# Attention, then two expert layers on one core: weight operands made on another engine, kept in DRAM for the second token sweep, and the gate rows and early routing re-spaced

## The chip, the cores and the metric

The kernel runs on one core of one Trainium2 chip. The metric is the device time of one execution in microseconds (us); a kernel's number is the median of its runs. One further execution was recorded by the hardware profiler; the rows below come from that one. Engines are named as the profile names them: PE (TensorE), PEld (its weight loads), DVE (VectorE), ACT (ScalarE), POOL (GpSimd), SP (SyncE, which here only issues DMAs).

## What is computed

Three layers in a row, cut here to what matters:

```python
x = linear_attention(q, k, v, lam)      # blocks with a decaying state; 1536 tokens of width 512
p = domain_probs / (domain_probs.sum(-1) + 1e-9)
out = 0
for e in range(4):                      # first expert layer: every token through every expert
    out += p[:, e:e+1] * (np.maximum(x @ w1[e], 0) @ w2[e])     # 512 -> 1024 -> 512
logits = out @ w_gate                   # second layer: 8 experts, one expert for each token
e_of = argmax(logits); gate = softmax(logits)[e_of]
y[mask] = gate[mask] * (np.maximum(out[mask] @ w1b[e], 0) @ w2b[e])
```

All of it in float32: each operand is split into a high and a low part in a shorter format, and a product is three matmuls (high by high, low by high, high by low).

## The kernel before

**Sweeps and units.** The first expert layer takes the tokens in two sweeps of 768 (`SW`, `TS`). In each sweep eight units run one after another, one for each half of the hidden width of each of the four experts: units k = 0 to 7 are the first sweep, 8 to 15 the second, and unit k + 8 needs the same weights as unit k. A unit has a first product (PE tiles `h` or `b`, then the hidden parts `ht`) and a second (`y`, added into `acc` token tile by token tile, six tiles a unit).

**Plain and fast units.** Units 0, 1, 8, 14 and 15 are plain: `moe1_group` takes 384 or 256 tokens at a time, four hidden chunks f (`h`), then token tiles (`y`); a callback `units(i)` places other work after each. Units 2 to 7 and 9 to 13 (`FAST`) form the first product from seven block products instead of eight; `fast_unit` runs 14 pieces (`line`), with `hook1(i)` after each, then six tiles `y`, with `hook2(j)` after each. The fast units need sums of blocks of tokens (`t1` to `t4`, made once a sweep in `tokens_steps` during units 1 and 8) and seven weight operands a unit: `a11`, `a12`, `a22` and the sums `s1` to `s4`.

**Making weight operands.** `load_piece` brings half a block (512 KB) into one of four `raw` buffers; `hi_lo` makes the parts: ACT copies the high one, DVE or POOL subtracts for the low one. For plain blocks and for all `w1` blocks (`split_plain`) the low part alternates between POOL and DVE. For the blocks of fast units (`fast_steps`) four sums `s` are made on POOL, and seven pairs of parts by ACT and DVE. `split_to(w, k, most)` takes the next `most` of these steps from one list; where the hooks call it sets the order on every engine, since the program is written out in the order in which each engine executes (`manual_schedule`). SP issues each DMA in program order and waits there for its buffer.

**Routing ahead of time.** For the first six token tiles `acc` is final after the first sweep. During the second, DVE computes their gate logits (`logit_v`, 48 products of 512 elements, eight gate rows fetched as two lots of four into `x2`). In units 14 and 15 each of these tiles then goes through `route_choose` (argmax) and, two steps later, `route_send` (softmax, rank and scatter): a pipeline that `route_step` moves on once a slot, a slot being a hidden chunk or a token tile. All six enter in the six slots of unit 14's first group.

After the two sweeps comes the second expert layer, which the change does not touch.

Of the kernel before, what the change touches and what calls it, by code (L numbers as in the profile page):

```python
# [8 lines left out]
F32 = mybir.dt.float32  # L9
# [9 lines left out]
P = 128  # L19
# [21 lines left out]
FAST = [k for k in range(2, K1 - 2) if k != KS]  # L41

# [20 lines left out]
def body(ctx: ExitStack, tc: tile.TileContext, lam, att, dp, w1a, w2a, wg, wgt, w1b, w2b, out):  # L63
# [61 lines left out]
    order = {b: i for i, b in enumerate(blocks)}  # L125
    wt = {}
# [6 lines left out]
    def load_piece():  # L133
        i = state["load"]
        if i >= 2 * len(blocks):
            return
        state["load"] += 1
        (w, k), j = blocks[i // 2], i % 2
# [32 lines left out]
    def split_plain(n, c):  # L171
        i, b = 4 * n + c, blocks[n]
        if c == 0:
# [10 lines left out]
        hi_lo(hi, lo, t, V if i in (0, 3) or n >= ROUTED else G if i < 3 else los[i % 2])  # L184
# [6 lines left out]

    def fast_steps(n):
        k = blocks[n][1]
        ops = wt[0, k] = {}
        got = {"n": 0}
        HH = HF // 2

        def raw(d, f):
            return raw_q[0 if d == 0 or got.get("dropped") else 1][:, :, f * HH:f * HH + HH]

        def part(name, src):
            i = got["n"]
            got["n"] += 1
            if i % 2 == 0:
                x = "hl"[i // 2 % 2]
                got["t"] = wp.tile([P, 4, HF], F32R, tag=f"w0{x}", name=f"w0{x}_{k}_{i}")
            ops[name] = tuple(
                got["t"][:, 2 * (i % 2) + x, :].rearrange("p (c f) -> p c f", c=2)
                for x in range(2)
            )  # L210
# [16 lines left out]
        return [
            lambda: part("a11", raw(0, 0)),
            lambda: part("a12", raw(1, 0)),
            lambda: add("s1", raw(0, 1), raw(1, 1), ALU.add),  # L230
            lambda: add("s2", got["s1"], raw(0, 0), ALU.subtract),
            lambda: part("s2", got["s2"]),
            lambda: part("s1", got["s1"]),
            lambda: add("s3", raw(0, 0), raw(0, 1), ALU.subtract),
            s3,
            lambda: part("a22", raw(1, 1)),
            s4,
            lambda: part("s4", got["s4"]),
        ]

# [7 lines left out]
    def split_to(w, k, most=1):  # L248

        for _ in range(most):  # L250
# [3 lines left out]
            if step is None:  # L254
                steps_q[:0] = [(n, x) for x in fast_steps(n)]
# [200 lines left out]
    def moe1_mm2(k, hs, t0, j, midway=None):  # L456
# [10 lines left out]
        mm3(ps, parts, not midway, True)  # L467
# [9 lines left out]
    def open_fast():  # L477
        fx = st["fx"] = st_ctx.enter_context(pool("fx", 1, side="right"))
        st["sf"] = st_ctx.enter_context(pool("sf", 2, side="right"))
# [12 lines left out]
    def tokens_steps(g):  # L492
        def sums(d):
# [19 lines left out]
            return ([] if g else [whole]) + [  # L513
# [14 lines left out]
    def fast_unit(k, hook1, hook2):  # L528
# [101 lines left out]
    def logit_load(h):  # L630
        w = x2.rearrange("p d t -> p (d t)")[:, :4 * DM].rearrange("p (e d) -> p e d", e=4)
        SP.dma_start(
            out=w, in_=wgt[4 * h:4 * h + 4, :].unsqueeze(0).to_broadcast([P, 4, DM])
        )

    def logit_v(t, e):
        flat = x2.rearrange("p d t -> p (d t)")
        V.tensor_tensor_reduce(  # L638
            out=flat[:, 4 * DM:5 * DM], in0=acc[:, t, 0:DM],
            in1=flat[:, e % 4 * DM:e % 4 * DM + DM], scale=1.0, scalar=0.0,  # L640
            op0=ALU.mult, op1=ALU.add, accum_out=lg_v[:, t, e:e + 1],
        )

# [197 lines left out]
    with tc.manual_schedule():  # L841
# [150 lines left out]
        def plain_unit(k):  # L992
            todo = tokens_steps(k // KS)
            base = k // KS * TS
            for g in range(2):
                def units(i):
                    if g == 0:
                        split_to(1, k)
                    if g == 1:
                        split_to(0, k + 1, 2 if i < FC or i == FC + 2 else 1)  # L1000
                    if todo and (g or i > 1):
                        todo.pop(0)()

                moe1_group(k, base + g * TH, TH, units)
            while todo:
                todo.pop(0)()
            split_to(0, k + 1, 11)

        logits = []
        for k in range(1, K1 - 2):  # L1010
            if k not in FAST:
                plain_unit(k)
                if k == KS:
                    logit_load(0)
# [467 lines left out]
```

## Time and profile before

| what | value |
|---|---|
| median of 3 runs (lowest to highest) | 778.96 us (777.73 to 779.73) |
| profiled execution: its own time | 777.45 us |
| its span, first to last instruction | 775.7 us |
| PE busy | 751.4 us (97%) |
| DVE, ACT, POOL busy | 497.3, 323.7, 200.7 us |
| mean granted clock of PE | 0.992 of full speed |

The profiled execution is 1.5 us under the median; 1.75 us of it lie outside the span. Busy time is an average over stages with different limits, so it says where the time is but not what a change of one stage is worth.

### The profile page before, as it was taken

How to read it: one execution, taken by the hardware profiler on the slowest of the kernel's cores; microseconds unless marked ns; L12 is line 12 of the kernel's file. 1: busy time of each engine (PE TensorE's matmuls, PEld its weight loads, DVE VectorE, ACT ScalarE, POOL GpSimd, SP SyncE). 2: the span in 40 equal slices, each digit the busy share in tenths (PEclk: the TensorE clock that was granted, in tenths of full speed). 3: DMA queues.
4: the chain of work that ended last, by engine and by line, in shares of the span. 5: the costliest groups of instructions: out<-in, count | busy, mean ns of one | idle time of the engine just before them, and what ended most of it. 6: DMA issues, size and time to landing. Idle time of an engine off the chain costs nothing.

```text
span 775.7 us, 12531 instructions
## 1 busy us (share of the span) xinstructions
PE 751.4 (97%) x4736; PEld 673.9 (87%) x4736; DVE 497.3 (64%) x1039; ACT 323.7 (42%) x692; POOL 200.7 (26%) x176
## 2 busy tenths in 40 slices
PE   8999989999999999989999899998999999999995
PEld 7888879898898998878889697986998999998994
DVE  6443285665655657556876878758446876765883
ACT  3222334252443434344343342522123656655673
POOL 4563251221321212312222231234110113211013
PEclk9999999999999999999999999999999999999998
DMA  9765101211122122122213122187004685855660
GB/s 298 254 213 164 55 13 70 75 62 57 53 81 82 55 81 82 55 65 76 78 55 128 35 82 72 64 302 242 28 15 142 223 296 202 300 170 201 233 236 29
DMA packets 29993, 97.43 MB, mean 126 GB/s; under 512 B 3633, under 2 KB 5681, under 8 KB 29675
## 3 DMA queue, kind: packets, MB, share of 16 engines
q1 hardware_dynamic: 27819, 90.30, 34.4%
q0 software_dynamic: 2112, 6.31, 2.1%
q8 instruction: 38, 0.62, 0.3%
q14 instruction: 24, 0.20, 0.1%
HBM read 85.55 MB, written 11.24 MB: 125 GB/s over the span
## 4 chain that ended last, share of the span: by engine, by line
PE 64%; issue 18%; DVE 9%; ACT 3%; POOL 2%; DMA 2%; SPq 1%; POOLq 0%; ACTq 0%; DVEq 0%
PE y L430 33%; PE b L554 16%; PE h L430 8%; POOL out L110 2%; PE qk L325 1%; DVE x L638 1%; PE xo L384 1%; PE xo L378 1%; DVE w1l L169 1%; DMA att<-in_att 1%; DVE u L568 1%; PE z L1139 1%; ACT w1h L168 1%; DMA x<-in_wgt 1%; DVE w0l L169 1%
## 5 line engine op out<-in xcount | busy, mean ns | idle before, releaser
L471 DVE SCALAR_TENSOR_TENSOR acc<-y,p_sb,acc 128x512 f32<-128x512 f32 x84 | 62.9, 749 | 47.6 <-PE y L430 47.2
L169 POOL TENSOR_TENSOR w1l<-raw,w1h 128x512 fp32r<-128x512 f32 x32 | 42.8, 1338 | 177.3 <-ACT w1h L168 177.3
L169 DVE TENSOR_TENSOR w1l<-raw,w1h 128x512 fp32r<-128x512 f32 x96 | 69.3, 750 | 14.2 <-ACT w1h L168 14.2
L168 ACT CAST w1h<-raw 128x512 fp32r<-128x512 f32 x128 | 75.4, 617 | 0.0
L168 ACT CAST w0h<-raw 128x512 fp32r<-128x512 f32 x117 | 66.8, 618 | 0.7 <-DMA raw<-in_w1b 0.6
L110 POOL DMA_INDIRECT out<-y,xb x16 | 29.3, 1833 | 135.8 <-DVE y L1255 84.9
L430 PE MATMUL h<-xh,w0h 128*128 128x256 f32 (+1 forms) x208 | 58.8, 312 | 1.2 <-ACT w0h L168 1.2
L430 PE MATMUL h<-xh,w0l 128*128 128x256 f32 (+1 forms) x208 | 56.9, 302 | 0.0
L561 ACT COPY u<-b 128x384 f32<-128x384 f32 x66 | 31.5, 478 | 53.9 <-PE b L554 53.9
L169 DVE TENSOR_TENSOR w0l<-raw,w0h 128x512 fp32r<-128x512 f32 x74 | 49.4, 707 | 7.0 <-ACT w0h L168 6.6
L554 PE MATMUL b<-xh,w0h 128*128 128x384 f32 x176 | 48.9, 339 | 0.0
L568 DVE TENSOR_TENSOR u<-b,u 128x384 f32<-128x384 f32 x66 | 36.5, 553 | 18.8 <-ACT w1h L168 11.7
L215 POOL TENSOR_TENSOR s<-raw 128x512 f32<-128x512 f32 x11 | 15.8, 1437 | 117.6 <-DVE w0l L169 117.6
L430 PEld LDWEIGHTS h<-xh,w0h 128*128 128x128 f32 x208 | 38.8, 191 | 2.8 <-ACT w0h L168 1.4
L638 DVE CUSTOM_DVE_ANT_0 x<-acc,x 128x512 f32<-128x512 f32 x48 | 37.3, 776 | 3.3 <-DMA x<-in_wgt 3.1
L430 PEld LDWEIGHTS h<-xh,w0l 128*128 128x128 f32 x208 | 39.0, 191 | 0.4
L430 PE MATMUL g<-xg,w0h 128*128 128x288 f32 (+1 forms) x192 | 38.1, 293 | 0.0
L430 PE MATMUL h<-xl,w0h 128*128 128x256 f32 (+1 forms) x208 | 37.4, 302 | 0.0
L554 PEld LDWEIGHTS b<-xh,w0h 128*128 128x128 f32 x176 | 32.3, 188 | 0.5
L430 PEld LDWEIGHTS h<-xl,w0h 128*128 128x128 f32 x208 | 31.6, 191 | 0.0
L430 PEld LDWEIGHTS g<-xg,w0h 128*128 128x128 f32 x192 | 30.8, 189 | 0.0
L110 POOL DMA_INDIRECT bins<-acc,pos x12 | 12.4, 1033 | 68.3 <-DVE acc L726 37.4
(303 smaller groups left out, 2146.5 us busy)
## 6 DMA issues: line engine op xcount, KB each, us to landing
raw<-in_w2a SPq DMA_DIRECT2D x32, 512.0 KB, 3.3
raw<-in_w1b SPq DMA_DIRECT2D x32, 512.0 KB, 5.6
raw<-in_w2b SPq DMA_DIRECT2D x32, 512.0 KB, 4.7
raw<-in_w1a SPq DMA_DIRECT2D x30, 512.0 KB, 3.5
att<-in_att SPq DMA_DIRECT2D x24, 512.0 KB, 5.6
bins<-fill SPq DMA_DIRECT2D x1, 4626.0 KB
x<-in_wgt SPq DMA_DIRECT2D x2, 1024.0 KB, 5.1
xb<-bins SPq DMA_DIRECT2D x2, 578.2 KB, 6.7
```

The source lines that it names most:

```text
L110: i = G.indirect_dma_start(out=dst, out_offset=bass.IndirectOffsetOnAxis(ap=idx, axis=0), in_=src, in_offset=None, bounds_check=rows - 1, ...
L168: A.copy(out=hi, in_=src)
L169: eng.tensor_tensor(out=lo, in0=src, in1=hi.bitcast(F32), op=ALU.subtract)
L215: G.tensor_tensor(out=t, in0=a, in1=b, op=op)
L325: T.matmul(qk[r][:, h, :], kT[64 * r:64 * r + 64, h, :], qT[64 * r:64 * r + 64, h, :], start=True, stop=True,)
L378: T.matmul(xo[q, h, :], st[q, h, :], qd[q, h, :], start=h == 0, stop=False, skip_group_check=True,)
L430: T.matmul(ps, l, r, start=first and i == 0, stop=last and i == len(ops) - 1)
L471: V.scalar_tensor_tensor(out=acc[:, t, 0:DM], in0=ps, scalar=p_sb[:, t, e:e + 1], in1=acc[:, t, 0:DM], op0=ALU.mult, op1=ALU.add,)
L554: T.matmul(ps, l[:, d, c], r[:, d, :], start=first and i == 0, stop=i == len(ops) - 1, skip_group_check=not first,)
L561: A.copy(out=t, in_=bank[2, s])
L568: V.tensor_tensor(out=t, in0=bank[b, s], in1=t, op=ALU.add)
L638: V.tensor_tensor_reduce(out=flat[:, 4 * DM:5 * DM], in0=acc[:, t, 0:DM], in1=flat[:, e % 4 * DM:e % 4 * DM + DM], scale=1.0, scalar=0.0, ...
```

## The change

Five edits. (1) The four sums of a fast block are made on DVE instead of POOL, first in the list, and the seven parts come in another order and pairing (`PAIRS`). (2) From unit 2 on, all low parts of plain blocks are made on DVE. (3) The finished operands of units 2 to 5 are also written to DRAM (`kept`, four DMAs a unit, 3.5 MB); units 10 to 13 (`KEPT`) fetch them back into the operand tiles instead of loading raw weights and making the parts again. (4) Gate rows come one at a time into a ring of five places, and logits are computed in units 10 to 13 alone, three among the pieces and two after each token tile. (5) The early tiles enter the routing pipeline every second slot. Besides: token steps of plain units start at slot 0, hooks take their steps at other slots, and the first `y` tile of a fast unit uses the low hidden parts last (`late="l"`).

```diff
+KEPT = [k for k in FAST if k >= KS and k - KS in FAST]
+PAIRS = (("a11", "a12"), ("a22", "s2"), ("s1", "s3"), ("s4",))
+    loads = [(w, k) for w, k in blocks if w or k not in KEPT]
...
-        hi_lo(hi, lo, t, V if i in (0, 3) or n >= ROUTED else G if i < 3 else los[i % 2])
+        hi_lo(hi, lo, t, V if i in (0, 3) or n >= ROUTED else G if i < 3 else los[i % 2] if k < 2 else V)
...
             hi_lo(*ops[name], src, V)
+            if j == len(PAIRS[i]) - 1 and k in kept:
+                m = 2 * len(PAIRS[i])
+                SP.dma_start(out=kept[k][i, :, :m], in_=t[:, :m].bitcast(F32))
...
-            G.tensor_tensor(out=t, in0=a, in1=b, op=op)
+            V.tensor_tensor(out=t, in0=a, in1=b, op=op)
...
         return [
+            sums,
             lambda: part("a11", raw(0, 0)),
             lambda: part("a12", raw(1, 0)),
+            third,
             lambda: part("s2", got["s2"]),
+            fourth,
+            lambda: part("s3", got["s3"]),
             lambda: part("s4", got["s4"]),
         ]
+    def kept_steps(n):
...
+            SP.dma_start(out=t[:, :m].bitcast(F32), in_=kept[k - KS][i, :, :m])
...
-                        split_to(0, k + 1, 2 if i < FC or i == FC + 2 else 1)
-                    if todo and (g or i > 1):
-                        todo.pop(0)()
+                        split_to(0, k + 1, 2 if i == FC - 1 else 1)
+                    step = todo.pop(0) if todo else None
+                    if step:
+                        step()
...
-                    logits = [(t, e) for h in range(2) for t in range(TT) for e in range(4 * h, 4 * h + 4)]
+                    logits = [(t, e) for e in range(E2) for t in range(TT)]
...
-                if i % 3 == 1:
+                if i % 2 == 0:
                     split_to(1, k)
-                elif i % 3 == 0:
+                elif i < 6 and k in KEPT:
                     logit(1)
...
-                logit(1)
+                if k in KEPT:
+                    logit(2)
...
+        early = [x for t in range(TT - 2) for x in (t, None)] + [TT - 2, TT - 1]
...
-                moe1_group(k, t0, n, units, range(TT) if t0 == TS and k == KL - 1 else ())
+                moe1_group(k, t0, n, units, early)
```

What stands where now, at three places. First DVE in the second group of plain unit 8, from the low part of its first hidden chunk to that of its last (`ht_1152_0l` to `3l`; `t` and `t3l`, `t2l`, `t4l` are a token step, `w0..` operands of unit 9, `s_9` its sums). Before:

```order
L438 SCALAR_TENSOR_TENSOR ht_1152_0l<-h_1152_0_3194,ht_1152_0h 128x384
L169 TENSOR_TENSOR w0h_0_3211<-raw_2968,w0h_0_3211 128x512
L169 TENSOR_TENSOR w0h_0_3211<-raw_2990,w0h_0_3211 128x512
L509 TENSOR_TENSOR t_1_1_3216<-x_96 128x384
L169 TENSOR_TENSOR t3l<-t_1_1_3216,t3h 128x384
L438 SCALAR_TENSOR_TENSOR ht_1152_1l<-h_1152_1_3220,ht_1152_1h 128x384
L509 TENSOR_TENSOR t_1_1_3241<-t_1_1_3216,x_96 128x384
L169 TENSOR_TENSOR t2l<-t_1_1_3241,t2h 128x384
L438 SCALAR_TENSOR_TENSOR ht_1152_2l<-h_1152_2_3245,ht_1152_2h 128x384
L169 TENSOR_TENSOR w0l_2_3262<-s_9_3239,w0l_2_3262 128x512
L169 TENSOR_TENSOR w0l_2_3262<-s_9_3237,w0l_2_3262 128x512
```

And now:

```order
L470 SCALAR_TENSOR_TENSOR ht_1152_0l<-h_1152_0_3222,ht_1152_0h 128x384
L229 TENSOR_TENSOR s_9_3239<-raw_2988,raw_3010 128x512
L229 TENSOR_TENSOR s_9_3241<-s_9_3239,raw_2988 128x512
L541 TENSOR_TENSOR t_1_1_3243<-x_100,t_1_1_3218 128x384
L172 TENSOR_TENSOR t4l<-t_1_1_3243,t4h 128x384
L470 SCALAR_TENSOR_TENSOR ht_1152_1l<-h_1152_1_3247,ht_1152_1h 128x384
L172 TENSOR_TENSOR w0h_0_3264<-raw_2988,w0h_0_3264 128x512
L470 SCALAR_TENSOR_TENSOR ht_1152_2l<-h_1152_2_3267,ht_1152_2h 128x384
L172 TENSOR_TENSOR w0h_0_3264<-raw_3010,w0h_0_3264 128x512
L470 SCALAR_TENSOR_TENSOR ht_1152_3l<-h_1152_3_3286,ht_1152_3h 128x384
```

Three token steps between the chunks became one; the other steps moved to the group before, where each of the four chunks now carries one. Second, DVE in unit 10 from the hidden part of piece (5, 1) to the start of the last sums (`x_96,lg_v` is a logit). Before:

```order
L438 SCALAR_TENSOR_TENSOR ht_111l<-u_10_3721,ht_111h 128x384
L638 ISA x_96,lg_v<-acc,x_96 128x512
L638 ISA lg_v 128x1
L438 SCALAR_TENSOR_TENSOR ht_100l<-b_10_3624,ht_100h 128x384
L169 TENSOR_TENSOR w1l_3644<-raw_3470,w1h_3643 128x512
L438 SCALAR_TENSOR_TENSOR ht_101l<-b_10_3634,ht_101h 128x384
L568 TENSOR_TENSOR u_10_3665<-b_10_3692,u_10_3665 128x384
```

And now:

```order
L470 SCALAR_TENSOR_TENSOR ht_111l<-u_10_3717,ht_111h 128x384
L470 SCALAR_TENSOR_TENSOR ht_100l<-b_10_3616,ht_100h 128x384
L470 SCALAR_TENSOR_TENSOR ht_101l<-b_10_3629,ht_101h 128x384
L600 TENSOR_TENSOR u_10_3661<-b_10_3687,u_10_3661 128x384
```

The logit and the low part of `w1` went to earlier pieces. Third, SP from the last loads ahead of unit 10 to the fetch for unit 11, now (before, each pair `raw<-in_w1a` stood where a lot of `kept` stands, and one `x<-in_wgt` of 2048 behind the second pair):

```order
L266 DMA w0h_0_3538<-kept_88 128x2048
L266 DMA w0l_1_3540<-kept_88 128x2048
L266 DMA w0h_2_3556<-kept_88 128x2048
L266 DMA w0l_3_3558<-kept_88 128x1024
L156 DMA raw_3653<-in_w2a 128x1024
L156 DMA raw_3696<-in_w2a 128x1024
L266 DMA w0h_0_3787<-kept_89 128x2048
L266 DMA w0l_1_3789<-kept_89 128x2048
L266 DMA w0h_2_3807<-kept_89 128x2048
L266 DMA w0l_3_3809<-kept_89 128x1024
L672 DMA x_100<-in_wgt 128x512 x2
```

Behind every fetch of four stand only loads for units further ahead and gate rows that are used more than a unit later.

## Rows read from the trace of the kernel before

**Rows 1.** Chain that ended last, in order of time: start, us, what.

```profile
122.59 14.69 PE b L554 x84
137.28 16.85 PE y L430 x72
...
366.34 0.60 DVE w1l L169
...
564.06 5.61 PE y L430 x24
...
583.93 5.75 PE h L430 x48
```

**Rows 2.** Busy time by stretch: start:end, length, PE, PEld, DVE, ACT, POOL; clock, DMA.

```profile
85.81:102.72 16.91, 16.91 (x85) 15.26 (x84) 7.97 (x13) 5.21 (x10) 6.87 (x7) 1.00 0.09 31
102.72:122.42 19.70, 17.43 (x85) 15.19 (x84) 16.07 (x24) 8.05 (x16) 9.98 (x7) 1.00 0.16 54
122.42:153.97 31.55, 31.55 (x158) 28.25 (x157) 19.24 (x29) 12.48 (x25) 7.86 (x6) 1.00 0.15 52
311.67:350.11 38.44, 36.36 (x169) 31.42 (x168) 21.22 (x33) 16.08 (x31) 9.07 (x6) 0.96 0.21 71
382.80:415.50 32.70, 32.12 (x157) 28.09 (x156) 26.23 (x52) 12.52 (x25) 8.20 (x6) 1.00 0.18 65
415.50:450.30 34.80, 32.34 (x158) 28.07 (x156) 26.25 (x52) 12.50 (x25) 8.18 (x6) 1.00 0.26 91
482.96:514.53 31.57, 31.57 (x157) 28.23 (x156) 20.34 (x39) 12.82 (x26) 9.74 (x18) 1.00 0.38 127
514.53:543.90 29.37, 25.92 (x156) 22.02 (x155) 22.16 (x100) 8.68 (x28) 11.51 (x10) 0.94 0.82 277
```

**Rows 3.** Timeline of unit 9, DVE, POOL and one weight load of PE.

```profile
362.47 1.28 POOL L215 TENSOR_TENSOR s<-raw,raw 128x512 f32<-128x512 f32 x1
362.69 1.48 DVE L438 SCALAR_TENSOR_TENSOR ht_111l<-u,ht_111h 128x384 fp32r<-128x384 f32 x1 [0.59 <-ACT ht_111h L437]
363.83 1.49 POOL L215 TENSOR_TENSOR s<-s,raw 128x512 f32<-128x512 f32 x1
364.09 1.77 DVE L638 CUSTOM_DVE_ANT_0 x<-acc,x 128x512 f32<-128x512 f32 x1
366.40 0.19 PEld L430 LDWEIGHTS y<-w1h,ht_100l 128*128 128x128 f32 x1 [0.68 <-DVE ht_100l L438]
```

**Rows 4.** Timeline of unit 13, DVE: the same two operations without POOL beside them.

```profile
495.53 0.56 DVE L438 SCALAR_TENSOR_TENSOR ht_111l<-u,ht_111h 128x384 fp32r<-128x384 f32 x1 [0.59 <-ACT ht_111h L437]
496.00 0.68 DVE L638 CUSTOM_DVE_ANT_0 x<-acc,x 128x512 f32<-128x512 f32 x1
```

**Rows 5.** Chain of waits within unit 8, second group.

```profile
335.89 0.48 DVE t L509
...
336.39 0.52 ACT t2h L168
...
336.94 0.56 DVE t2l L169
337.50 0.47 DVE ht_2l L438
```

**Rows 6.** Busy time by stretch, of two us each.

```profile
344.00:346.00 2.00, 2.00 (x6) 1.57 (x5) 0.69 (x1) 0.49 (x1) 0.00 (x0) 0.50 0.00 0
522.36:524.37 2.01, 1.88 (x9) 1.39 (x10) 1.77 (x15) 0.53 (x2) 0.00 (x0) 1.00 1.15 345
```

**Rows 7.** Timeline of unit 11: DVE at the second lot of gate rows.

```profile
426.42 0.69 DVE L638 CUSTOM_DVE_ANT_0 x<-acc,x 128x512 f32<-128x512 f32 x1 [2.06 <-DMA x<-in_wgt]
```

**Rows 8.** Timeline of units 14 and 15, first groups.

```profile
534.39 0.17 PE L701 MATMUL rank<-oh,upper 128*128 128x8 bf16 x1 [2.46 <-DVE oh L673]
535.86 2.29 DVE L169 TENSOR_TENSOR w1l<-raw,w1h 128x512 fp32r<-128x512 f32 x1
```

**Rows 9.** Page, part 6: DMA issues, KB each, median us from issue to landing.

```profile
x<-in_wgt SPq DMA_DIRECT2D x2, 1024.0 KB, 5.1
```

More of the change, by code (lines that the diff above doesn't have):

```diff
@@ L134, in load_piece @@
         i = state["load"]
[L135 removed]
+        if i >= 2 * len(loads):
             return
         state["load"] += 1
[L138 removed]
+        (w, k), j = loads[i // 2], i % 2
         if k < K1:
@@ L183, in split_plain, with pair_of @@
             hi, lo = hi[:, c, :], lo[:, c, :]
-        hi_lo(hi, lo, t, V if i in (0, 3) or n >= ROUTED else G if i < 3 else los[i % 2])
+        hi_lo(hi, lo, t, V if i in (0, 3) or n >= ROUTED else G if i < 3 else los[i % 2] if k < 2 else V)
         if c % 2 == 1:
             drop_raw()
+    kept = {
+        k: dram.tile([len(PAIRS), P, 4, HF], F32, name=f"kept{k}") for k in FAST if k + KS in KEPT
+    }
+    def pair_of(t, j):
+        return tuple(
+            t[:, 2 * j + x, :].rearrange("p (c f) -> p c f", c=2) for x in range(2)
+        )
     def fast_steps(n):
@@ L194, in fast_steps @@
         ops = wt[0, k] = {}
-        got = {"n": 0}
+        got = {}
         HH = HF // 2
+        d0, d1 = raw_q[:2]
         def raw(d, f):
-            return raw_q[0 if d == 0 or got.get("dropped") else 1][:, :, f * HH:f * HH + HH]
+            return (d0, d1)[d][:, :, f * HH:f * HH + HH]
         def part(name, src):
[L202 to L205, printed above, removed]
+            i, j = next((i, p.index(name)) for i, p in enumerate(PAIRS) if name in p)
+            if j == 0:
+                x = "hl"[i % 2]
@@ L232, in fast_steps, with fetch @@
             lambda: part("s2", got["s2"]),
[L233 to L237, printed above, removed]
+            fourth,
+            lambda: part("s3", got["s3"]),
             lambda: part("s4", got["s4"]),
         ]
+    def kept_steps(n):
+        k = blocks[n][1]
+        ops = wt[0, k] = {}
+        def fetch(i):
+            x = "hl"[i % 2]
+            t = wp.tile([P, 4, HF], F32R, tag=f"w0{x}", name=f"w0{x}_{k}_{i}")
+            names = PAIRS[i]
+            m = 2 * len(names)
+            SP.dma_start(out=t[:, :m].bitcast(F32), in_=kept[k - KS][i, :, :m])
+            for j, name in enumerate(names):
+                ops[name] = pair_of(t, j)
+        return [lambda i=i: fetch(i) for i in range(len(PAIRS))]
@@ L466, in moe1_mm2 @@
             parts = parts[FC // 2:]
-        mm3(ps, parts, not midway, True)
+        mm3(ps, parts, not midway, True, late)
         if k % KS == 0:
@@ L588, in fast_unit @@
             q, o = divmod(j * P, TH)
-            moe1_mm2(k, [hs[q, f] for f in range(FC)], t0 + q * TH, o // P)
+            moe1_mm2(
+                k, [hs[q, f] for f in range(FC)], t0 + q * TH, o // P, late="r" if j else "l"
+            )
             hook2(j)
```

69 lines of the change are left out of this document (36 added, 33 removed).

## The prediction

> **What bounds the kernel now.** I read the stretches between the starts of units first. PE is the bound wherever nothing holds it: a plain group of 384 tokens takes 16.91 us with PE busy throughout, a fast unit of the first sweep 31.55 us, the same; so does unit 13 with 31.57 [rows 2]. The chain of waits gives the two halves of a fast unit, 14.69 and 16.85 us [rows 1]. Against these lengths the other stretches show what PE lost:
>
> - unit 1, second group: 19.70, lost 2.8 [rows 2];
> - unit 8, both groups: 38.44 instead of 33.82, lost 4.6 [rows 2];
> - units 9, 10 and 12: 32.7 each (unit 10 is shown, the others are within 0.04), lost 1.15 each, and unit 11 34.80, lost 3.25: together 6.7 [rows 2];
> - the first groups of units 14 and 15: 29.37. Undisturbed groups further on have 5.75 + 5.61 = 11.36 [rows 1], two of them 22.7, and some 0.3 of rank matmuls stays: lost 6.35 [rows 2].
>
> Together 20.5 us, all in stretches that the change edits. In each, timelines and chain name DVE as what PE waits for: a hidden low part in unit 9 [rows 3], the chain through token steps in unit 8 [rows 5], the choice `oh` in unit 15 [rows 8]. The first sweep's six fast units lose nothing, so edits there can only cost.
>
> **Why DVE is late.** In unit 9 two sums `s` run on POOL from 362.47 on; the low part beside them takes 1.48 us and the logit behind it 1.77, and PE's load waits for the next low part [rows 3]. In unit 13, whose successor needs no sums, the same two operations take 0.56 and 0.68 [rows 4], and the unit loses nothing, though it has logits too. So 2.0 us of DVE's time are waits for POOL, and they cost 1.15 of PE's. Which instructions suffer is told by the rows as well: those with both inputs in SBUF. The Trainium skill, page "SBUF — State Buffer", section "Who interferes with whom", says that the second read port is shared, held for a whole instruction, and that a DVE instruction with two SBUF inputs blocks against a POOL instruction that reads SBUF. By that rule a sum moved to DVE cannot meet anything, since no POOL arithmetic is left after unit 1; the rows agree (1.77 beside 0.68), and the 2.0 would vanish whole. Were the port merely shared in proportion, part of it would stay with the added DVE work; that belongs to the second rival.
>
> **The change part by part.**
>
> *Sums and low parts to DVE (edits 1, 2).* Per fast unit four sums and two low parts more, about 0.6 us each by the low part in the chain [rows 1]: 3.6 us. A first-sweep unit has DVE busy for 19.24 of 31.55 [rows 2], some 2 of it waits of the above kind; afterwards about 21. PE hides it. Were that cover gone, it would cost at most 3.6 in each of six units.
>
> *Kept operands (edit 3).* In units 10 to 13 DVE loses seven low parts (4.2 us), ACT as many copies. The price is 3.5 MB written in each of units 2 to 5 and 3.5 MB fetched in units 9 to 12. Nothing waits for a store before its tile is reused a unit later. A fetch can begin when PE has read the old tile, the last one at the end of the first half (14.69), and is needed from 31.55 on, the last tile 12.6 later still (12 of 14 pieces). No row shows such a fetch; the nearest is 1,024 KB from DRAM in 5.1 us [rows 9], so four one after another take 18, within the 16.85 plus the pieces ahead of each use. From below it costs nothing; I take nothing. From above: unit 11 shows 91 GB/s in all [rows 2]; at only that rate 3.5 MB take 38 us (the rival on the other side).
>
> *Gate rows by a ring (edit 4).* In unit 11 DVE stood 2.06 us until the second lot landed [rows 7]; with it unit 11 lost 2.1 more than its neighbours. In the ring the sixth row is asked for in unit 10 and used in unit 12. That stall goes. Unit 9 has no logits; units 10 to 12 have 15 instead of 11, but only three among the pieces, all ahead of the seventh. DVE per unit: 26.2 [rows 2], less 4.2 of parts, less about 2.4 of waits, plus 1.2 for two low parts and 2.7 for four logits: 23.5 of 31.55. After piece 6 nothing but hidden parts is queued, and `late="l"` asks for the low parts eight matmuls into the tile instead of after one. I take units 9 to 13 at 31.6 each: 6.5 of the 6.7 come back. Bounds: 2.1 (the stall alone) to 6.7.
>
> *Plain units 1 and 8.* A token step holds DVE for 0.48, then waits for ACT's 0.52 and another 0.56: 1.6 us, with the hidden part's 0.47 [rows 5]. A slot of the second group had that and two steps of `w0`, 0.47 + 1.2 + 1.6 = 3.3 us, against PE's 2.1 for a chunk (12 matmuls, where the chain has 84 in 14.69 [rows 1]). In unit 8 two of three such token steps go elsewhere, so the second group should wait for nothing. What is late next is its first group: four slots of hidden part, one low part and a token step, 0.47 + 0.6 + 1.6 = 2.67. Walked through from the first low part (2.9 us in: a chunk, ACT's high part and the hand-overs), three slots later the fourth high part comes at about 11.05, where PE wants it at 8.5 + 6 x 0.234 = 9.9 (0.234 is 16.85 / 72 [rows 1]), and the low part lags a further 0.3: 1.5 lost. Unit 8 gets back 3.1. Unit 1's second group keeps two token steps in the first four slots but one step of `w0` in each instead of two; the same walk gives the fourth high part at 10.45 for 9.9: 0.9 lost, 1.9 back. Bounds: 0 to 2.8 for unit 1. For unit 8 at best 4.6; at worst the new pause pulls the clock down: after the old one the granted clock was 0.50, that is 1.2 GHz, at 344 to 346 [rows 6], eight matmuls cost 1.6 more, and only 1.5 comes back.
>
> *Early routing (edit 5).* One send and one choice take DVE 2.01 us [rows 6]. In unit 14's first group fell five choices and three sends, and low parts on POOL made DVE stand again: one on DVE took 2.29 beside one on POOL [rows 8], and two such waits more are of 1.2 and 0.6. DVE lagged until PE waited 2.46 for `oh` [rows 8]; the granted clock of the stretch is 0.94 [rows 2]. Now the group has three choices and two sends. DVE's 22.16 us over the two groups [rows 2] lose about 3.4 of waits and a send (1.0) that slips to the third group, and gain four low parts (2.4): 20.2 in 23.0. Slot by slot, group one (11.5 us) ends without a stall; DVE is at a send, a choice and a low part until 14.8, though the next hidden part is there at 13.35, and makes up for it until the third low part, 0.45 late. Lost 0.5 instead of 6.35: 5.9 back. Bounds: 2 (a wait of 2.5 and the half clock stay) to 6.3.
>
> **The sum.** 1.9 + 3.1 + 6.5 + 5.9 = 17.4 us. The profiled execution's 777.45 becomes 760.0; it stands 1.5 under the median of 778.96, and from that the same sum gives 761.6. I say **762**. All bounds at their worst give 0 + 1.5 + 2.1 + 2.0 = 5.6 (773), at their best 20.4 (758.6). A measurement of this kernel can tell about 0.3%, 2.3 us.
>
> **Rivals.**
>
> 1. *The plain and routing stretches stay DVE's* (0.19). DVE is full to 88% there by my own count. If PE still pauses for 2 to 3 us in units 8 and 15 and falls to half clock after each (1.6 each), 6 to 8 of the 17.4 go: 768 to 770. For it: DVE and ACT wait for each other in every token step [rows 5]. Against: no POOL wait is left.
>
> 2. *DVE becomes the bound of the second sweep* (0.12). The skill's page "Perfetto Trace Analysis", section "Optimizing Scalar/DVE Operations", advises handing work of a saturated DVE to another engine, even POOL; this change does the reverse, with DVE busy for 26.2 of 32.7 us. As a mechanism of this kernel: the 15 logits and four low parts before the seventh piece hold up the hidden sums, and each of units 10 to 12 keeps its 1.15: 765; or 768 if the ring's loads stall DVE as before. Against: unit 13 lost nothing with DVE at 20.3 [rows 2], and 4.2 us of parts leave.
>
> 3. *Slower: fetches come late* (0.04). SP issues in order, and a fetch that waits for PE holds up what is behind. If operands move at the 91 GB/s of unit 11, one unit's 3.5 MB and 1 MB of `w1` take 49 us, against 38 from the release of the first old tile (6 of 14 pieces, 6.3) to the last use (31.55 + 12.6): 11 or more lost in each of four units, 44 less the 17.4: about 805. It decides from 4.4 us late per unit. Against: DMA ran at 277 GB/s over the first routing groups [rows 2].
>
> 4. *No change* (0.02), 777 to 781: the second expert layer, where nothing is edited, would have to lose what is won here.
>
> **Chances.** The forecast, 759 to 765, has 0.63. With rivals 1 and 2 up to 770 that is about 0.9; the range 759 to 770 leaves out rival 3 and the tails. Faster 0.93, same 0.03, slower 0.04.
>
> **What the profile would show.** Fast units 9 to 13 at 31.6 each, with no DVE operation over 0.8 us among the pieces; unit 8's first group at about 18.4 and the second at 16.9; the first groups of 14 and 15 at about 23.5; POOL without arithmetic after unit 1; fetches landing before the unit that uses them. A `y` that waits for `ht_3h` in unit 8 for over 2 us, or a clock under 1.00 behind it, would show rival 1; a PE wait on a fetched `w0h` rival 3.

## The result and the profile after

The changed kernel takes **762.0 us** (761.4 to 762.2), the kernel before 779.3 beside it: a ratio of 0.978 [0.976, 0.980]. The profiled execution took 761.43 us with a span of 759.6, where before had 777.45 and 775.7, so the profiles account for 16.0 of the 17.3 us. The first two rows are part 1 of the page after; the rest is busy time by stretch, with the columns of [rows 2].

```profile
span 759.6 us, 12447 instructions
...
PE 744.5 (98%) x4736; PEld 671.7 (88%) x4736; DVE 491.6 (65%) x1073; ACT 307.6 (40%) x664; POOL 92.6 (12%) x98
```

```profile
102.67:120.58 17.91, 17.42 (x85) 15.17 (x84) 13.17 (x24) 7.04 (x15) 0.83 (x1) 1.00 0.39 150
120.58:152.12 31.54, 31.54 (x157) 28.24 (x156) 22.92 (x38) 12.96 (x26) 0.00 (x0) 1.00 0.54 201
152.12:183.66 31.54, 31.54 (x157) 28.24 (x156) 21.29 (x35) 12.57 (x25) 0.00 (x0) 1.00 0.50 186
309.82:328.35 18.53, 17.17 (x86) 15.22 (x84) 11.78 (x22) 8.02 (x16) 0.00 (x0) 1.00 0.17 57
328.35:345.25 16.90, 16.90 (x85) 15.26 (x84) 10.05 (x17) 7.80 (x15) 0.00 (x0) 1.00 0.26 72
345.25:376.80 31.55, 31.55 (x157) 28.25 (x156) 14.39 (x24) 9.74 (x20) 0.00 (x0) 1.00 0.50 187
376.80:408.47 31.67, 31.67 (x158) 28.22 (x156) 22.58 (x50) 8.47 (x18) 0.00 (x0) 1.00 0.43 159
408.47:440.13 31.66, 31.66 (x157) 28.22 (x156) 23.89 (x54) 8.47 (x18) 0.00 (x0) 1.00 0.44 165
503.47:527.38 23.91, 23.48 (x153) 20.62 (x152) 19.52 (x90) 8.43 (x26) 4.08 (x4) 1.00 0.98 328
```

In order of the second fence: unit 1's second group (19.70 before), units 2 and 3, the two groups of unit 8 (38.44 together), units 9, 10 and 11 (32.69, 32.70 and 34.80), and the first groups of units 14 and 15 (29.37) [rows 2]. Every stretch that had lost time has come down, no fast unit of the first sweep has grown, and the clock is 1.00 in all of them, also in the routing groups, where it was 0.94. The columns of DVE and POOL show the trade: unit 3, like units 4 to 6, has DVE at 21.3 us where a fast unit of the first sweep had 19.2 to 19.3, and POOL at 0.00 where it had 7.86 (unit 2 has 22.92, since work left over from unit 1 falls into it); units 10 and 11 have DVE at 22.6 and 23.9 instead of 26.2.

What PE still waits for between 85 and 553 us is this list (what, us in total, times, the longest):

```profile
PE y L462 <- ACT w1h L171: 1.4, 1, 1.4
PE rank L741 <- DVE oh L713: 0.4, 1, 0.4
PE y L462 <- ACT ht_3h L469: 0.3, 1, 0.3
PE y L462 <- DVE ht_3l L470: 0.2, 1, 0.2
```

The first wait is unit 8's first group; the second is in the routing groups, where one of 2.46 stood [rows 8]; the last two are unit 1's. No wait for a fetched operand is among them. The DMA issues between 345 and 480 us, KB each and median us from issue to landing, tell what a fetch takes:

```profile
w0h<-kept SPq DMA_DIRECT2D x8, 1024.0 KB, 6.8
w0l<-kept SPq DMA_DIRECT2D x4, 1024.0 KB, 7.6
w0l<-kept SPq DMA_DIRECT2D x4, 512.0 KB, 8.5
```

### The profile page after: what moved, and what is told of

Its sections match the earlier page's. It is cut to its first block, busy times and chain, and to the rows that moved or that the text cites. A ratio compares the mean times of both kernels' runs of the same rounds, so it can differ in the third digit from the quotient of the medians.

```text
span 759.6 us, 12447 instructions
## 1 busy us (share of the span) xinstructions
PE 744.5 (98%) x4736; PEld 671.7 (88%) x4736; DVE 491.6 (65%) x1073; ACT 307.6 (40%) x664; POOL 92.6 (12%) x98
## 4 chain that ended last, share of the span: by engine, by line
PE 87%; issue 4%; DVE 4%; DMA 2%; SPq 1%; ACT 1%; POOL 0%; POOLq 0%; ACTq 0%
PE y L462 35%; PE b L586 21%; PE h L462 9%; PE g L462 5%; PE z L462 3%; PE zr L1255 2%; PE qk L357 1%; PE z L1179 1%; PE xo L416 1%; PE xo L410 1%; DMA att<-in_att 1%; PE g L1179 1%; DVE w1l L172 1%; PE gr L462 1%; PE xt L1161 1%
## 5 line engine op out<-in xcount | busy, mean ns | idle before, releaser
L172 DVE TENSOR_TENSOR w1l<-raw,w1h 128x512 fp32r<-128x512 f32 x124 | 82.6, 689 | 16.8 <-ACT w1h L171 16.5
L172 DVE TENSOR_TENSOR w0l<-raw,w0h 128x512 fp32r<-128x512 f32 x80 | 51.6, 684 | 6.6 <-ACT w0h L171 6.0
L171 ACT CAST w0h<-raw 128x512 fp32r<-128x512 f32 x98 | 55.7, 619 | 0.2
L677 DVE CUSTOM_DVE_ANT_0 x<-acc,x 128x512 f32<-128x512 f32 x48 | 32.9, 685 | 0.6
L586 PE MATMUL b<-xl,w0h 128*128 128x384 f32 x88 | 29.9, 339 | 0.0
L1179 PE MATMUL z<-g,w1h 128*128 128x352 f32 (+2 forms) x96 | 29.1, 366 | 0.7 <-DVE g L1201 0.6
```

Source lines behind the costliest of these rows:

```text
L171: A.copy(out=hi, in_=src)
L172: eng.tensor_tensor(out=lo, in0=src, in1=hi.bitcast(F32), op=ALU.subtract)
L586: T.matmul(ps, l[:, d, c], r[:, d, :], start=first and i == 0, stop=i == len(ops) - 1, skip_group_check=not first,)
L677: V.tensor_tensor_reduce(out=x2.rearrange("p d t -> p (d t)")[:, RING * DM:], in0=acc[:, t, 0:DM], in1=logit_piece(e), scale=1.0, scalar=0 ...
L1179: T.matmul(ps[:, :2 * n], wh, both, start=i == 0, stop=False)
```

## The experiments

The table gives the stretches of all kernels that tell something there, in us, each read from the start of one unit to the start of the next. "Routing" is the first group of units 14 and 15 each and the one behind them, 503.47 to 541.86 in the changed kernel.

| kernel | unit 1, 2nd group | unit 8 | units 9 to 13 | routing |
|---|---|---|---|---|
| before | 19.70 | 38.44 | 164.4 | 43.62 |
| changed | 17.91 | 35.43 | 158.2 | 38.39 |
| e1, work back to POOL | 17.91 | 35.27 | 157.7 | 42.25 |
| e2, nothing kept | 17.93 | 35.44 | 166.1 | 38.40 |
| e3, two lots | 17.92 | 35.45 | 159.9 | 38.50 |
| e4, routing in a row | 17.93 | 35.45 | 158.1 | 42.19 |
| e5, before with the move alone | 19.19 | 39.36 | 162.3 | 42.05 |
| e10, old places in plain units | 22.36 | 42.20 | 158.2 | 38.40 |
| e7, four edits | 16.90 | 33.82 | 157.7 | 38.83 |
| e8, three edits | 16.90 | 33.82 | 157.7 | 38.63 |

**e1: the work back to POOL.** The four sums and every second low part go back; all else stays.

```diff
-        hi_lo(hi, lo, t, V if i in (0, 3) or n >= ROUTED else G if i < 3 else los[i % 2] if k < 2 else V)
+        hi_lo(hi, lo, t, V if i in (0, 3) or n >= ROUTED else G if i < 3 else los[i % 2])
...
-            V.tensor_tensor(out=t, in0=a, in1=b, op=op)
+            G.tensor_tensor(out=t, in0=a, in1=b, op=op)
```

> The changed kernel with the four sums and every second low part given back to POOL; kept operands, ring and spread routing stay. By the theory of the prediction (a POOL operation that reads SBUF stretches the small DVE operations beside it to two or three times their time, and both engines are late after it): DVE operations with two SBUF inputs go from 0.56 to about 1.5 us and from 0.68 to about 1.8 us where they meet POOL; unit 1 loses 0.5 to 1 us again, unit 8 1 to 2 us, the second sweep's units 9 to 13 0.3 to 1 us each (POOL has 2 low parts in each, and the sums of unit 9), the first groups of 14 and 15 1 to 2 us. Sum +4 to +8 us, 766 to 770. Rival A (the time came from keeping operands, the ring and the spacing; which engine takes sums and low parts does not matter): 761.5 to 763. Rival B (DVE's load is what counts, POOL is relief): 758 to 761.

765.3 us (764.2 to 765.6), ratio 0.982 [0.980, 0.984]. Of the places where a loss was expected only the routing shows it. Unit 10, by stretch, and the routing:

```profile
377.08:408.62 31.54, 31.54 (x157) 28.24 (x156) 21.62 (x48) 8.75 (x18) 2.60 (x2) 1.00 0.43 160
...
503.25:545.50 42.25, 39.51 (x257) 35.09 (x255) 28.82 (x134) 11.83 (x38) 13.31 (x12) 0.96 0.59 205
```

In units 10 to 13 POOL has two low parts and no sums, since kept operands need none; PE loses nothing, even 0.12 us less per unit than in the changed kernel. In the routing it loses 3.9 us. The timeline there (start, us, engine) shows how:

```profile
519.27 1.43 DVE L755 SCALAR_TENSOR_TENSOR pf<-rk_all,ec,far 128x1 f32<-128x1 f32 x1
...
519.37 1.30 POOL L172 TENSOR_TENSOR w1l<-raw,w1h 128x512 fp32r<-128x512 f32 x1
...
521.25 1.92 DVE L709 SCALAR_TENSOR_TENSOR sc<-lg_v,mx,desc 128x8 f32<-128x8 f32 x1
...
521.87 1.27 POOL L172 TENSOR_TENSOR w1l<-raw,w1h 128x512 fp32r<-128x512 f32 x1
...
523.68 0.17 PE L741 MATMUL rank<-oh,upper 128*128 128x8 bf16 x1 [2.75 <-DVE oh L713]
```

A DVE instruction on one element per partition takes 1.43 us and one on eight takes 1.92; in the changed kernel the same two take 0.22 and 0.23:

```profile
520.09 0.22 DVE L755 SCALAR_TENSOR_TENSOR pf<-rk_all,ec,far 128x1 f32<-128x1 f32 x1
...
520.85 0.23 DVE L709 SCALAR_TENSOR_TENSOR sc<-lg_v,mx,desc 128x8 f32<-128x8 f32 x1
```

In e1 each ends 0.03 us after a POOL low part. The second began before that low part, beside a scatter that POOL issued; why it did not end ahead of the low part, no row shows. They lead to `oh`, PE waits 2.75 us for it, and the granted clock is 0.50 (1.2 GHz) until 527.3.

**e2: nothing kept.** Units 10 to 13 make their operands again.

```diff
-    loads = [(w, k) for w, k in blocks if w or k not in KEPT]
+    loads = blocks
...
-                make = kept_steps if blocks[n][1] in KEPT else fast_steps
+                make = fast_steps
```

> The changed kernel without kept operands: units 10 to 13 make their seven operands again on ACT and DVE from blocks loaded anew, nothing is written to DRAM in the first sweep. By the theory (keeping is what gives DVE the room that the logits need): DVE in units 10 to 13 rises from 23 to some 29.5 to 30.5 us of 31.67, work queues up behind the logits, and PE waits 1 to 3 us in each unit; sum +4 to +10 us, 766 to 772. Rival (without POOL beside it DVE has room for both, the keeping is not needed): units 10 to 13 stay at 31.6 to 31.8 us, total 761 to 763.

770.1 us (769.7 to 770.4), ratio 0.989 [0.987, 0.990]. Unit 11 by stretch (units 12 and 13 are within 0.02 of it), PE's waits from unit 11 to 13, and DVE in unit 12, which starts at 443.44:

```profile
409.14:443.44 34.30, 32.41 (x158) 28.16 (x156) 30.16 (x66) 12.36 (x25) 0.00 (x0) 1.00 0.24 77
```

```profile
PE b L586 <- ACT u L593: 5.3, 6, 1.0
```

```profile
449.71 0.55 DVE L600 TENSOR_TENSOR u<-b,u 128x384 f32<-128x384 f32 x1
```

The first hidden sum `u` starts 6.3 us into the unit; in the changed kernel's unit 11 it starts 3.6 in (412.03). DVE is not full, 30.16 of 34.30 us, but the logits and `acc` additions of the tiles of the unit before are still in its queue, and the work with a due time stands behind them. PE then waits for a bank of PSUM that ACT can't copy out, because ACT waits for DVE. Keeping is worth 7.9 us here, and it is a DVE bound, not a POOL one: POOL is at 0.00.

**e3: gate rows in two lots.** `logit_lot` loads four gate rows in one DMA, the second lot once the first has been used.

```diff
-        if t == TT - 1:
-            logit_load(e + RING)
+        if (t, e) == (TT - 1, 3):
+            logit_lot(1)
...
-                    for e in range(RING):
-                        logit_load(e)
-                    logits = [(t, e) for e in range(E2) for t in range(TT)]
+                    logit_lot(0)
+                    logits = [(t, e) for h in range(2) for t in range(TT) for e in range(4 * h, 4 * h + 4)]
```

> The changed kernel with the gate rows again in two lots of four, the second loaded when the last logit of the first is done. By the prediction the ring is worth the wait for the second lot in unit 11: logits stand still for a load of about 5 us (1024 KB in the trace of before), DVE's low parts behind them come late and PE loses about 2 us there, nothing elsewhere: +1.5 to +2.5 us, 763 to 764.5. Rival (with operands kept DVE has slack enough to take a stop of 5 us): PE's loss in unit 11 under 0.3 us, 761.5 to 762.5.

763.6 us, one run. Unit 12 has 33.33 us instead of 31.67, and all other stretches are as they were. The first row is DVE's stop for the second lot, at the end of unit 11; the second is the only wait listed for PE from unit 10 to 13, 12 us into unit 12:

```profile
439.19 0.69 DVE L683 CUSTOM_DVE_ANT_0 x<-acc,x 128x512 f32<-128x512 f32 x1 [3.38 <-DMA x<-in_wgt]
```

```profile
PE b L586 <- ACT u L593: 1.0, 1, 1.0
```

So loading row by row into the ring is worth 1.7 (the logits keep their new places in e3), inside the expected 1.5 to 2.5, though DVE stands for 3.4 us in a unit that has 8 us to spare: what it could not do at the end of unit 11 is ahead of unit 12's hidden sums, and PE pays a unit later than named.

**e4: routing in a row.**

```diff
-        early = [x for t in range(TT - 2) for x in (t, None)] + [TT - 2, TT - 1]
+        early = list(range(TT))
```

> The changed kernel with the six early token tiles started in consecutive slots again. By the theory (a slot with choice, placing and row of three tiles holds more DVE work than PE takes for a slot; the spacing spreads it): PE loses 1.5 to 2.5 us more in the first groups of 14 and 15, waiting for one-hot rows and ranks, 763.5 to 764.5. Rival (the waits there came from POOL's low parts beside the small operations, and the spacing does nothing): first groups 23.5 to 24.3 us as now, 761.5 to 762.5.

766.2 us, one run. PE's three longest waits in the routing:

```profile
PE rank L741 <- DVE oh L713: 1.2, 1, 1.2
PE rank L741 <- DVE df L720: 1.0, 1, 1.0
PE y L462 <- DVE ht_3l L470: 0.9, 2, 0.6
```

Routing goes from 38.39 to 42.19, twice the expected loss. Together with e1 this tells what gained the 5.2 us there: the spacing alone (e1) gives 1.4, the move of low parts alone (e4) 1.4, both give 5.2. Neither alone explains the gain: with one of them left out, DVE lags long enough for PE to stop.

**e5: before, with the move alone.** The same two lines as in e1, turned round, in the kernel before.

> The kernel before with one edit alone: the four sums, and the low parts of plain blocks from unit 2 on, go from POOL to DVE; nothing is kept, lots of four, routing in consecutive slots, the old order of steps. By the prediction's cause (in units 9, 10 and 12 it is DVE's waits for POOL that cost PE 1.15 us each): these three come to 31.6 to 31.8 us, unit 11 keeps only its stop for the second lot, 33 to 33.8; the first groups of 14 and 15 gain 1.5 us or more; total 770 to 774. Rival (DVE is late there because it has too much to do, with or without POOL; keeping operands is what helped): 3.6 us of DVE work more per unit leave units 9, 10 and 12 at 32.7 or longer, to 34, and the second group of unit 8 at 21 or longer; total 777 to 783.

778.8 us (775.8 to 780.8), ratio 1.001 [0.999, 1.003]: no change. Unit 8's second group and units 9 to 12:

```profile
329.12:351.04 21.92, 19.47 (x85) 16.33 (x84) 11.91 (x21) 8.84 (x17) 0.00 (x0) 0.92 0.20 59
351.04:382.90 31.86, 31.84 (x158) 28.21 (x157) 24.87 (x52) 12.94 (x26) 0.00 (x0) 1.00 0.20 76
382.90:414.63 31.73, 31.73 (x157) 28.22 (x156) 27.27 (x58) 12.47 (x25) 0.00 (x0) 1.00 0.18 67
414.63:450.09 35.46, 33.37 (x158) 29.74 (x156) 28.20 (x59) 12.56 (x26) 0.00 (x0) 0.95 0.24 89
450.09:481.65 31.56, 31.56 (x157) 28.20 (x156) 26.63 (x57) 12.52 (x25) 0.00 (x0) 1.00 0.19 68
```

Units 9, 10 and 12 come to 31.86, 31.73 and 31.56 with DVE doing more in them than before (27.27 us in unit 10, 26.23 before [rows 2]). So the prediction's cause for these three units holds: all but 0.31, 0.18 and 0.02 of their 1.15 us were POOL's. The total was missed, and so was unit 11, expected at 33 to 33.8: the rival's loss is real too, elsewhere. Unit 8's second group grows from 21.00 to 21.92 and unit 11 from 34.80 to 35.46, its clock at 0.95 behind a wait of 2.1. In the profiled run 1.9 us of gain remain, 773.8 for 775.7; over ten runs none does. That profile is of the fastest of the ten: where the median run loses 3 us more stands in no trace.

**e6: what of POOL's work DVE feels.** Work that serves nothing, in two units of the changed kernel.

```diff
+            if k in (11, 12):
...
+                G.tensor_copy(out=st["pc"], in_=hs[j, 2 * i + s][1][:, :1].bitcast(F32))
+                if k == 11:
+                    G.tensor_tensor(out=pb, in0=pa, in1=pa, op=ALU.add)
+                else:
+                    G.memset(pb, 0.0)
+                    G.memset(pb, 0.0)
```

> The changed kernel with POOL work that serves nothing and changes no output: after each of the eight hidden low parts of unit 11 POOL adds a 128x512 tile to itself (it reads and writes SBUF), in unit 12 it fills such a tile twice (it only writes); unit 10 is left as it is. By the lock (the Trainium skill, page SBUF — State Buffer, section Who interferes with whom: only a POOL operation that reads SBUF contends with a DVE operation with two SBUF inputs): in unit 11 logits of 0.69 us, low parts of w1 of 0.69 and hidden low parts of 0.56 take up to 1.7 us where they overlap an addition, while those with one input in PSUM (acc 0.75, u 0.55) keep their time; in unit 12 all are as in unit 10. PE loses up to 1 us in unit 11 and nothing in unit 12. Rival (any POOL work beside DVE slows it, by writes or by sharing bandwidth): both units show longer DVE operations, those with an input in PSUM too. Total 761.5 to 763.5.

763.0 us, one run; unit 11 takes 32.37 us, unit 12 31.73, unit 10 31.67. Timeline, first two pairs from unit 11, then one from unit 12:

```profile
414.79 1.50 POOL L606 TENSOR_TENSOR pb<-pa 128x512 f32<-128x512 f32 x1
...
415.42 1.41 DVE L172 TENSOR_TENSOR w1l<-raw,w1h 128x512 fp32r<-128x512 f32 x1
...
423.27 1.04 POOL L606 TENSOR_TENSOR pb<-pa 128x512 f32<-128x512 f32 x1
...
423.39 0.54 DVE L470 SCALAR_TENSOR_TENSOR ht_101l<-b,ht_101h 128x384 fp32r<-128x384 f32 x1
...
447.11 0.68 DVE L690 CUSTOM_DVE_ANT_0 x<-acc,x 128x512 f32<-128x512 f32 x1
...
447.17 0.53 POOL L608 MEMSET pb<- 128x512 f32 x1
```

The low part of `w1`, two inputs in SBUF, goes from 0.69 to 1.41 us and ends 0.54 after POOL's addition, nearly its own length. POOL's addition takes 1.50 where it began beside a logit and 1.04 where it had DVE's PSUM operations for company. A hidden part with one input in PSUM (`b`) keeps 0.54 within an addition, and a logit beside a fill keeps 0.68. That is what was expected by the lock, and what the Trainium skill says, page "SBUF — State Buffer", section "Who interferes with whom": a DVE operation with two SBUF inputs against a POOL operation that reads SBUF, the later one waiting out the earlier. The trace agrees on all three cases. DVE loses about 2.2 us by eight additions (logits 0.755 instead of 0.686 on average, low parts 0.87 instead of 0.69, two hidden parts), PE 0.7.

**e10: old places in the plain units.**

```diff
-            return ([] if g else [whole, None]) + [
+            return ([] if g else [whole]) + [
...
-                        split_to(0, k + 1, 2 if i == FC - 1 else 1)
-                    step = todo.pop(0) if todo else None
-                    if step:
-                        step()
+                        split_to(0, k + 1, 2 if i < FC or i == FC + 2 else 1)
+                    if todo and (g or i > 1):
+                        todo.pop(0)()
...
-            assert not any(todo)
+            while todo:
+                todo.pop(0)()
```

> The changed kernel with the old places in the plain units alone: token steps from the third slot on and the rest behind the unit, two steps of w0 in each of the first slots of the second group; the sums are on DVE, nothing is on POOL. By the prediction's walk through the slots (the places are what unit 8 gained by): unit 8 has 17.4 + 20.5 to 22 us again, unit 1's second group 19 to 19.8; total 766 to 768. Rival (POOL's sums beside the token steps were the cause, and they are gone): unit 8 at 35 to 36, unit 1's second group under 18.3, total 761.5 to 763.

773.1 us, one run. Unit 1's second group and unit 8's, by stretch, PE's longest waits in the whole run (2.8 us in each of the two units), and one later us of unit 8:

```profile
102.91:125.27 22.36, 19.22 (x85) 16.29 (x84) 16.61 (x29) 7.92 (x16) 3.66 (x3) 0.92 0.56 212
331.96:356.71 24.75, 20.58 (x86) 17.12 (x85) 12.39 (x22) 9.26 (x18) 0.00 (x0) 0.86 0.32 97
```

```profile
PE y L462 <- ACT ht_3h L469: 5.7, 2, 2.8
```

```profile
350.00:351.00 1.00, 1.00 (x4) 0.73 (x3) 0.00 (x0) 0.58 (x1) 0.00 (x0) 0.50 1.05 367
```

Unit 8 loses 6.8 us and unit 1 4.5, each over 2.5 more than the upper end of what was expected. A slot of the second group holds a hidden part, two steps of `w0` and a token step again, and PE waits for the fourth hidden part; the half clock costs once more, from 346.0 to 352.8 in unit 8. The excess can be placed beside e5, which has the old places and the old, smaller steps, with the sums on DVE: 39.36 in unit 8 and 19.19 in unit 1. A step of the new list is two operations of DVE where it had been one (`sums` two sums, `third` and `fourth` a part and a sum), so two in a slot can be more than two of the old. The new places, with the new steps in them, are what gained unit 8's 3.0 us, not the engine: with both new unit 8 takes 35.43 with the sums on DVE and 35.27 with them on POOL (e1), with both old 39.36 and 38.44 (e5, before).

**e7 and e8: can the remaining losses go?** e7 makes four edits of the changed kernel, e8 takes two of them over and puts `w0` elsewhere in unit 1.

```diff
-        hi_lo(hi, lo, t, V if i in (0, 3) or n >= ROUTED else G if i < 3 else los[i % 2] if k < 2 else V)
+        hi_lo(hi, lo, t, V if i in (0, 3) or n >= ROUTED else G if i < 3 else los[i % 2] if k < KL - 1 else V)
...
-                split_to(k + 2 == KL, k + 1, 2)
+                split_to(k + 2 == KL or k + 1 == KS, k + 1, 2)
...
-                        split_to(0, k + 1, 2 if i == FC - 1 else 1)
+                        split_to(0, k + 1, (1, 0, 0, 1, 2, 2, 2)[i])
```

In e7 the tuple was (0, 0, 0, 1, 2, 2, 3) and the early tiles were 0, 1, 2, 3 every second slot, then two empty slots, 4, one empty, 5.

> The changed kernel with four small edits where it still loses time: the low parts before unit 14 alternate between POOL and DVE again (those of units 14 and 15 stay on DVE); w1 of unit 8 is made in the second half of unit 7; in unit 1 the steps of w0 come later in the second group; the early tiles 4 and 5 start later. If each loss has the cause read from the traces: unit 8's first group 18.53 to about 17 (-1.5), unit 1's second group 17.91 to about 17.1 (-0.8), units 10 to 13 31.67 to 31.54 (-0.5), the first groups of 14 and 15 -0.4: 758.5 to 760. Rival (the work only moves: unit 7 or the start of unit 2 takes the loss, POOL's low parts meet the logits): 761.5 to 763.

760.3 us (759.9 to 760.5), ratio 0.977 [0.974, 0.979]. Unit 8 and units 10 to 13 do as expected. In unit 1 the rival was right: the second group is at 16.90, and unit 2 takes what it had saved,

```profile
119.92:152.51 32.59, 31.80 (x158) 28.18 (x156) 24.16 (x40) 13.91 (x28) 2.63 (x2) 1.00 0.68 257
```

because ACT's copy of a bank stands behind a `w0` cast that waits for a late sum on DVE. The early tiles did not gain: the routing takes 38.83, beside 38.39 in the changed kernel here and 38.6 in e9 below.

> The changed kernel with three small edits: low parts before unit 14 alternate between POOL and DVE, w1 of unit 8 is made in the second half of unit 7, and in unit 1's second group the eight steps of w0 lie in the slots as 1, 0, 0, 1, 2, 2, 2 (the two sums in the idle first slot, nothing beside the hidden parts). The early tiles stay as the change has them. If the causes read from the traces hold: unit 8 33.82 (-1.6), unit 1's second group and unit 2 together 48.45 to 48.7 instead of 49.46 (-0.8 to -1.0), units 10 to 13 31.54 each (-0.5), the first groups of 14 and 15 as in the changed kernel: 2.9 to 3.1 us less than it on the same chip. Rival (unit 1's work only moves into unit 2, as the later steps did): 2.0 us less.

759.0 us (758.9 to 759.4), ratio 0.974 [0.971, 0.977]. Unit 1's second group, unit 2 and unit 8's first group:

```profile
103.09:119.99 16.90, 16.90 (x85) 15.26 (x84) 12.15 (x22) 6.93 (x14) 0.85 (x1) 1.00 0.17 63
119.99:151.56 31.57, 31.57 (x157) 28.25 (x156) 24.27 (x38) 13.09 (x27) 2.66 (x2) 1.00 0.69 254
...
309.26:326.17 16.91, 16.91 (x86) 15.26 (x84) 9.48 (x18) 6.19 (x12) 0.00 (x0) 1.00 0.01 3
```

Units 10 to 13 take 31.54 each. Unit 1's second group and units 2 to 13 now have PE's own length, with only a few hundredths left over.

**e9: the changed kernel beside e8.**

> The changed kernel as it is, on the chip on which the two beside it run: 761.5 to 762.5, and the same stretches.

762.3 us (761.9 to 762.5), its stretches as in the profile after to within 0.03, routing 0.2 longer. So e8 gains 3.3 us on it on one chip, with no overlap of the runs: 1.0 in unit 1, 1.6 in unit 8, 0.4 in units 10 to 13 by the stretches.

## Why the prediction was right, point by point

The time, 762.0, is the one named, to the tenth by luck: between the medians, 779.3 and 762.0, the gain is 17.3 us, but between the two profiled executions, from which the sum of 17.4 was read, it is 16.0: 0.1 short in units 1 and 8 each, 0.3 in units 9 to 13, 0.45 in the first groups of 14 and 15; 0.2 was lost in the second layer, and some tenths lie elsewhere.

- **What bounds it.** Right: PE everywhere, and DVE what it waited for. The fast units of the first sweep kept 31.54 us. DVE's forecast for them, about 21, was right too: units 3 to 6 have 21.3. The 2 us of waits were there and went: in unit 3 before, `ht_111l` took 1.49 us, two low parts of `w1` 1.00 each and one of `w0` 1.12; now they take 0.56, 0.69 and 0.68. PE had never paid for them.
- **Kept operands.** Hidden, as taken. A fetch of 1,024 KB takes 6.8 to 7.6 us where the nearest row had 5.1 [rows 9], and the half-size last one 8.5; one after another they would be some 30 us and not 18. But a unit's four are under way together: those for unit 11 are issued from 387.3 to 391.8, and with 10.0 us, the longest of any transfer from or to `kept`, the last would land by 402, ahead of the unit's start at 408.5. So nothing waits, for another reason than the one given.
- **Why DVE is late in units 9, 10 and 12.** Right as a cause, but for the change only half of the story. The waits for POOL were nearly all of the 1.15 (e5); that they were the port's and not ACT's waits for late sums is read from [rows 3] and from e6, where additions on POOL that nothing needs cost PE 0.7 in a unit. Yet keeping removes the sums from these units, whoever makes them, and the two low parts that are left on POOL do no harm there (e1, e8). Had the change left both on POOL, units 9 to 13 would have been 0.5 us better; the 6.5 needed edits 3 and 4, not edits 1 and 2, which alone gave 2.1 (e5, in its fastest run). The sum did not show this, because it took all edits of a stretch together. Of edit 4 only the loading was taken back alone (e3): what the logits' new places and `late="l"` are worth, no run shows.
- **The 0.12 in each of units 10 to 13** was in no term. By the timeline, logits and low parts of `w1` come ahead of a hidden sum on DVE, which starts 9.99 us into unit 10; ACT's next copies stand behind it, the last of them ends at 388.26, and PE starts a matmul of piece (4, 1) 0.1 late at 388.60. With two of the unit's four low parts on POOL (e1) the sum starts 9.45 in and the 0.12 is gone.
- **Ring.** 1.7 by e3, where the row had 2.06 [rows 7].
- **Unit 8.** 18.53 and 16.90 for the forecast 18.4 and 16.9; e1 and e10 show that places and steps did it. (In the kernel before, DVE's third token step, `t` and `t4l`, and `ht_3l` came behind the last line of the first order list; PE waited 1.47 us for `ht_3h` there.) The wait named was wrong: in the first group now PE did not wait for `ht_3h` but for the high part of `w1`'s fourth chunk, made behind it on ACT. ACT in this group, and PE:

```profile
319.76 0.51 ACT L171 CAST t2h<-t 128x384 fp32r<-128x384 f32 x1 [1.26 <-DVE t L541]
320.18 0.48 ACT L469 ACTIVATE ht_3h<-h 128x384 fp32r<-128x384 f32 x1
...
320.56 0.61 ACT L171 CAST w1h<-raw 128x512 fp32r<-128x512 f32 x1
...
321.23 0.50 PE L462 MATMUL y<-w1h,ht_3h 128*128 128x512 f32 x1 [1.36 <-ACT w1h L171]
```

  ACT's queue stands while it waits 1.26 us for DVE's token sum; the token cast, the hidden part and the cast that PE needs follow. The walk had followed DVE's queue and stopped at the hidden part. That this cast starts only 0.4 us behind the hidden part made the number right, by luck. The walk's own terms do not quite give its figure either: 2.9 and three slots of 2.67 are 10.9, not 11.05, and the 10.45 for unit 1 cannot be worked out from what is given. In e7 and e8 the 1.6 is gone; their low parts on POOL give little of it (e1, with `w1` still in place, has 18.37), so moving `w1` into unit 7 gave the rest.
- **Early routing.** 23.91 for 23.5. The wait left, 0.43, has the size forecast (0.45), again by luck: it is for a choice's `oh` in unit 15's first group, not for the third low part. It was the one place where taking work off POOL mattered for the change (e1): 1.4 us without the spacing (42.19 in e4 for 43.62 before), 3.9 with it (38.39 for 42.25 in e1).
- **Rivals.** The first did not come, but its mechanism is seen where edits are taken back: a wait of 2.75 us in e1's routing and of 2.8 in e10's unit 8, then the half clock. The second is what e2 shows, 2.6 us in each of units 11 to 13; keeping is what stood against it. The advice quoted there is hedged in the Trainium skill, page "Perfetto Trace Analysis", section "Optimizing Scalar/DVE Operations": it goes on that between these two engines handing work over might not help, since they share a read port. For the third nothing spoke in any run.

What the single edits cost when taken back is 3.3 (e1), 8.1 (e2), 1.6 (e3), 4.2 (e4) and 11 (e10) us by the times, against 762.0 (single runs for e3, e4 and e10): 28 in all, or 27 against the 762.3 of e9 on the chip on which all five ran, where the change as a whole gains 17. The edits are not terms of a sum; each one's worth depends on the others' being there. What stays open is the exact share of step size and step place in e10: no run has the old steps at the new places.

## What to carry to other kernels

Look for what is queued ahead of the work with a due time on the engine, not for the engine's share: DVE cost PE time when busy for 30 of 34 us (e2), for 12 of 18.5 (unit 8) and for 22 of 29 (routing before), and almost none at 27 of 32 (e5, unit 10). When two edits both relieve one queue, test them one at a time in both directions, taken back from the new kernel and put alone into the old one: here one direction alone would have said that the move to DVE is worth nothing (e5), and the other that it is worth 3.3 us (e1), and both are true. Before moving work off POOL everywhere, see where small operations with a waiter meet it: two low parts a unit on POOL were free, four in the routing, two of them beside its operations of one and eight elements, cost 3.9 us.

## What was not expected of the hardware

- A small DVE operation can lose as much beside POOL as a large one: one element per partition took 1.43 us for 0.22, eight took 1.92 for 0.23 (e1). Operations of 384 and 512 elements lost 0.7 (e6), 0.9 and 1.1 [rows 3, rows 4] and 1.6 us [rows 8]. In the routing the small ones lead to `oh`, for which PE waits.
- Pauses of PE of 1.36 us (changed, unit 8) and 1.0 us (e3) left the granted clock at 1.00. After one of 2.1 (e5, unit 8) or 2.75 (e1) it fell to 0.50 some 1.4 and 0.2 us after PE had begun again, and stayed there for 3.4 us both times. In e10's unit 8 (pauses of 1.2 and 2.8) it fell 0.7 us before PE began again, and stayed for 6.8. The length of the pause alone does not tell what follows: in the kernel before, pauses of 1.7 and 0.6 in unit 1 left the clock at 1.00, and 1.5 and 0.6 in unit 8 were followed by 0.50 from 342.8 to 346.2.
- The times scatter with the pauses: before and e5 range over 5 to 6 us on one chip (777.4 to 783.5, 775.8 to 780.8), the changed kernel and e8 over 0.6 to 0.8. The clocks listed with these runs go from 0.987 to 0.995 in the first two and from 0.996 to 0.998 in the others; that the scatter comes from there is argued, not tested.
